# RWKV-6 attention and an MLP: products with A and with the state in two operations, standard deviation behind the MLP, a new order

## The chip, the cores and the metric

The kernel runs on one core of a Trainium2 chip, as one launch. The metric is the device time of one execution in microseconds (us), from three runs: lowest, median and highest. Beside them stands one execution taken by the hardware profiler.

## The reference

Two blocks follow each other. The first is a recurrence over time, for 4 batches and 8 heads of width 48, with 768 steps. Each head keeps a 48 x 48 state:

```python
for t in range(S):
    kt, vt, rt, wt = (k[:, :, t], v[:, :, t], r[:, :, t], w[:, :, t])
    cur = np.einsum('bhd,bhe->bhde', u[None] * kt, vt)
    y[:, :, t] = np.einsum('bhd,bhde->bhe', rt, state + cur)
    state = wt[:, :, :, None] * state + np.einsum('bhd,bhe->bhde', kt, vt)
```

The heads are then laid side by side (8 x 48 = 384 columns), and the second block is a residual MLP behind a layer norm without an offset, 384 to 1536 and back:

```python
xn = (x - mu) / np.sqrt(var + 1e-06) * g_ln
ch = np.maximum(xn @ w_ch1, 0.0) @ w_ch2
return x + ch
```

All data is fp32.

## The kernel before

**Rounds, units, tiles.** The work is cut into 8 rounds (4 batches x 2 halves of 384 steps). A round has two units of four heads, and three tiles of 128 steps; a tile holds two chunks of 64 steps for each head. Two heads lie on one tile's partitions, one on rows 0 to 47 and one on rows 64 to 111, so most products of the attention use a quarter of TensorE's array (48 or 64 rows by 48 to 64 columns), and four of them are put side by side. Such operations are called tiled here; a run of them is a burst. Round 0 is worked on in two parts, tile 0 and then tiles 1 and 2, to have the first results early (`parts_of_round`).

**The attention of a part** (`front`, L1675). `load` (L559) fetches w, k and r from HBM. `inner` (L583) forms on VectorE or GpSimd, in groups of four steps, what these steps do to each other (tiles `rk`, `pad_k`, `pad_r`, `nat_k`, `nat_w`, summed into `vals`), and `inner_by_tile` sends the sums through HBM into the layout of a masked copy. `turn` and `turn_w` transpose k, r and w on TensorE, ScalarE evicts them. Then come levels 2 to 5: at each, `quads` multiplies k by r for pairs of blocks of 4, 8, 16, 32 steps (PSUM tile `a`), `grow` (L850) multiplies k and r by the decay of a block on VectorE, and `keep` (L879) copies the wanted blocks of `a` into the matrix `A` (steps by steps, within a chunk) under a mask, on VectorE; `keep_last` does level 5 on ScalarE, and `place_own` puts the sums of `inner` on the diagonal. `turn_k` transposes k again, `load_v` fetches v, and a copy `vx` with the halves of the partitions swapped. `states` (L997) multiplies k by v for each chunk and scans the results into the states `s`, on VectorE.

**Outputs.** `outputs` (L1073) is one tiled operation for a unit. For each of its pairs of heads and tiles it issues four products with `A` (64 rows) and four products of r with the state (48 rows), which add up in one PSUM tile. Where both operands must lie on the same partitions as the result's other terms, it reads swapped copies: `rx` of r (made by `exchange_r`, L916) and `sx` of the state (made at the end of `states`), both on ScalarE, some 36 copies each in the whole kernel.

**Layer norm and MLP.** `normalize` (L1149) computes mean and variance on VectorE, the square root on ScalarE and the reciprocal on VectorE (`rstd`), and then xn = (x - mean) x rstd on VectorE. `turn_x` (L1219) transposes xn on TensorE, and ScalarE evicts it times g (`xf`). In round 0 the MLP's first product is in fp32 (`first_product`). From round 1 on it is made of three products in fp32r: operands are split into a high part, a low part and a difference (tiles `xhl`, `xd`; the weights `wh`, `wl`, and `d`, which is streamed from HBM by SP for each of the 12 column blocks). In rounds 4 to 7 the second product is split as well (`thirds`, L1461; `hH`, `hL`, `hD`). In the other rounds `mlp` (L1583) makes it in fp32 (PSUM tile `o`). VectorE adds the result to x, and SP stores it.

**The order.** No loop order of the program is the order of issue. Each piece is recorded with `plan.add`: which engines may do it and for how long, what it reads and writes, and which buffers it needs. `Plan.order` (L242) then walks a written list, `ORDER` (L76), of the recorded operations' numbers (plus 10000 where the second of the possible engines does it, 20000 for the third), gives each its buffers, and issues it. All engines issue in program order through one helper, `InOrder.call` (L47); so every instruction has line L47 in the profile, and is told by its tiles. Where the plan expects TensorE to wait for over 0.35 us and a bank of PSUM of kind `b` is free, it puts in products of zeros (`idle`, L1773), which nobody reads. `port` tells that VectorE and GpSimd are kept from working at the same time in such an operation.

**Start.** GpSimd builds the masks (`build_mask`, L486, and `build_own_mask`, L499) by selections on an index pattern and copies; VectorE clears `vals` and both PSUM tiles of kind `a`. The two buffers `A0` and `A1` are cleared once by an operation of the plan, on ScalarE, GpSimd or VectorE.

Of the kernel before, what the change touches and what calls it, by code (L numbers as in the profile page):

```python
# [55 lines left out]
class Op:  # L56
    def __init__(self, i, costs, fn, pri, lat, size, port, tiled, count):
        self.i, self.costs, self.fn, self.pri = i, costs, fn, pri
        self.lat, self.size, self.port, self.tiled, self.count = lat, size, port, tiled, count
        self.need, self.new, self.uses = set(), [], set()  # L60
        self.start = self.end = self.eng = None


class Plan:
# [177 lines left out]
    def order(self, busy, idle=None):  # L242
# [37 lines left out]
        for entry in self.ORDER:  # L280
# [55 lines left out]
            for n in op.uses:  # L336
                users[n] -= 1
                last[n] = max(last.get(n, 0.0), op.end)
                if not users[n]:
                    self.homes[self.tile_tag[n]].append((last[n] + self.RELEASE, self.place[n]))  # L340
# [1474 lines left out]
```

## Time and profile before

| what | value |
|---|---|
| three runs, lowest / median / highest | 489.94 / 490.76 / 492.56 us |
| profiled execution, own time | 490.19 us |
| its span, first to last instruction | 488.5 us |
| granted TensorE clock, mean | 1.000 |
| VectorE busy | 366.7 us (75%) |
| ScalarE busy | 274.0 us (56%) |
| GpSimd busy | 113.1 us (23%) |
| moved by DMA | 56.23 MB |

PE is TensorE's matmul, PEld its weight load, DVE VectorE, ACT ScalarE, POOL GpSimd, SP the engine that issues most transfers. A row of a timeline gives the start in the span, the busy time, the engine, line and operation, the tile written and those read with their shapes, the number of records, and, in brackets, the idle time ahead of it and what ended that. An fp32 product shows as two records. A row of the groups has the form, the number of records, their busy time and the mean of one in ns, and the idle time of the engine ahead of them.

### The profile page before, as it was taken

To read this page: it belongs to the slowest core of one execution; us is meant where nothing else is said; L and a number is where in the kernel's file an instruction comes from. 1 tells how busy PE (TensorE), PEld (TensorE's weight loads), DVE (VectorE), ACT (ScalarE), POOL (GpSimd) and SP (SyncE) were. 2 spreads that over 40 slices of the span, in tenths; PEclk is the share of its full clock that TensorE was granted. 3 is DMA by queue.
4 is the path that set the end of the run, shared out by engine and by line. 5 is a ranking of instruction groups with operands and counts; after the bars stand their busy time and mean duration, and the time that the engine had idled before them with its cause. 6 is when DMAs were issued, how large, how long until landed. Compare 5 with 4: busy or idle time off the path is not lost.

```text
span 488.5 us, 17306 instructions
## 1 busy us (share of the span) xinstructions
PE 477.8 (98%) x7412; PEld 410.4 (84%) x7412; DVE 366.7 (75%) x753; ACT 274.0 (56%) x624; POOL 113.1 (23%) x120
## 2 busy tenths in 40 slices
PE   8898999999999999999999999999999999999996
PEld 5676988767987778986699867799999999999996
DVE  6999999999966996875837998688887622732545
ACT  5779978943674256564064534779864444434430
POOL 4614013201602307404000610100141022121130
PEclk9999999999999999999999999999999999999999
DMA  7866777578452574461275403533411312223101
GB/s 210 237 174 148 205 176 171 163 177 218 126 150 75 96 208 94 115 186 39 70 201 140 90 3 58 109 116 85 125 34 60 88 47 65 66 66 98 64 1 49
DMA packets 105469, 56.23 MB, mean 115 GB/s; under 512 B 61872, under 2 KB 102320, under 8 KB 105392
## 3 DMA queue, kind: packets, MB, share of 16 engines
q1 hardware_dynamic: 105120, 54.92, 43.3%
q8 instruction: 58, 0.95, 0.9%
q10 hardware_dynamic: 272, 0.20, 0.1%
q14 instruction: 19, 0.16, 0.1%
HBM read 45.27 MB, written 7.47 MB: 108 GB/s over the span
## 4 chain that ended last, share of the span: by engine, by line
PE 87%; DVE 5%; SPq 1%; issue 1%; DMA 1%; DVEq 0%
PE h_ps L47 33%; PE a L47 23%; PE o L47 18%; PE o_2P L47 3%; PE r_ps L47 2%; PE o_2D L47 2%; PE xT_ps L47 2%; PE k_ps L47 2%; PE kn_ps L47 2%; SPq L47 1%; DVE A L47 1%; DVE s L47 1%; DVE x L47 1%; DVE k L47 1%; DMA d<-w1d 1%
## 5 line engine op out<-in xcount | busy, mean ns | idle before, releaser
L47 PE MATMUL o<-ffn,h 128*128 128x384 f32 x288 | 99.2, 488 | 0.0
L47 ACT ACTIVATE h<-h_ps 128x384 f32<-128x384 f32 (+2 forms) x108 | 47.7, 454 | 54.8 <-PE h_ps L47 54.2
L47 PEld LDWEIGHTS o<-ffn,h 128*128 128x128 f32 x288 | 52.3, 190 | 29.1
L47 ACT ACTIVATE h_ps<-h_ps 128x384 f32<-128x384 f32 x84 | 38.8, 475 | 49.0 <-PE h_ps L47 47.0
L47 DVE SCALAR_TENSOR_TENSOR hD<-hH,hL 128x384 fp32r<-128x384 f32 x48 | 30.4, 651 | 34.8 <-PE a L47 16.9
L47 PE MATMUL h_ps<-xd,d 128*128 128x384 f32 x204 | 50.0, 353 | 0.3 <-DMA d<-w1d 0.3
L47 PEld LDWEIGHTS a<-r,k 48*56 48x56 f32 (+3 forms) x3072 | 39.7, 122 | 10.1 <-issue 3.1
L47 POOL TENSOR_TENSOR hL<-h,hH 128x384 fp32r<-128x384 f32 x24 | 26.8, 1127 | 86.8 <-PE o_2D L47 21.1
L47 PE MATMUL a<-r,k 48*56 48x32 f32 (+3 forms) x3072 | 44.1, 208 | 1.1 <-DVE k L47 0.9
L47 PE MATMUL h_ps<-xhl,wl 128*128 128x384 f32 x180 | 43.8, 351 | 0.0
L47 DVE TENSOR_TENSOR k<-k,tot 112x768 f32<-112x768 f32 (+1 forms) x40 | 37.8, 947 | 5.9 <-PE a L47 4.5
L47 PE MATMUL h_ps<-xhl,wh 128*128 128x384 f32 x180 | 41.4, 338 | 0.0
L47 PEld LDWEIGHTS h_ps<-xd,d 128*128 128x128 f32 x204 | 35.4, 188 | 2.9 <-issue 0.9
L47 DVE TENSOR_TENSOR r<-r,tot 112x768 f32<-112x768 f32 (+1 forms) x40 | 34.1, 854 | 0.6 <-PE a L47 0.2
L47 PEld LDWEIGHTS h_ps<-xhl,wh 128*128 128x128 f32 x180 | 32.3, 188 | 0.0
L47 PEld LDWEIGHTS h_ps<-xhl,wl 128*128 128x128 f32 x180 | 31.0, 188 | 1.1 <-ACT h_ps L47 0.2
L47 PE MATMUL idle<-nought 128*128 128x384 f32 (+1 forms) x96 | 28.7, 425 | 1.0 <-DVE eps L47 1.0
L47 ACT ACTIVATE hH<-h 128x384 fp32r<-128x384 f32 x48 | 24.4, 522 | 8.0 <-PE a L47 3.5
L47 DVE COPY_PREDICATED A<-mask,a 128x768 f32<-128x768 int8 (+2 forms) x27 | 24.1, 893 | 5.6 <-PE a L47 5.5
L47 PE MATMUL h_ps<-xf,w 128*128 128x128 f32 (+1 forms) x144 | 26.0, 331 | 0.0
L47 PEld LDWEIGHTS idle<-nought 128*128 128x128 f32 x96 | 17.3, 200 | 9.1 <-issue 1.5
L47 DVE TENSOR_TENSOR hL<-h,hH 128x384 fp32r<-128x384 f32 x24 | 14.5, 606 | 13.7 <-PE o_2P L47 5.0
(180 smaller groups left out, 1171.2 us busy)
## 6 DMA issues: line engine op xcount, KB each, us to landing
d<-w1d SPq DMA_DIRECT2D x84, 192.0 KB, 2.8
raw<-in_moe_w_ch_dram SPq DMA_DIRECT2D x24, 384.0 KB, 3.9
nat_r<-in_r_dram SPq DMA_DIRECT2D x24, 192.0 KB, 4.0
nat_w<-in_w_dram SPq DMA_DIRECT2D x24, 192.0 KB, 4.2
v<-in_v_dram SPq DMA_DIRECT2D x24, 192.0 KB, 4.1
nat_k<-in_k_dram SPq DMA_DIRECT2D x23, 192.0 KB, 3.9
w1d<-w1diff SPq DMA_DIRECT2D x12, 192.0 KB, 3.4
out_dram<-x SPq DMA_DIRECT2D x4, 576.0 KB, 4.6
```

The source lines that it names most:

```text
L47: ins = self.tc.keep_in_program_order(f(*args, **kw))
```

## The change

In eight parts:

1. `exchange_r` and the swapped copy of the state are gone. `outputs` is split: `inside` issues the products with `A`, and `outputs` those of r with the state, now with the rows of r and of the state where they lie. Between both stands an operation of GpSimd, a memset of one element (`token`), which waits for the products with `A` and for which those with the state wait; `Op.after` adds these waits by hand.
2. xn is now mean - x, without rstd, and may be made on ScalarE or VectorE. g is negated once at the start. rstd multiplies the MLP's result in the addition of x; in rounds 4 to 7 ScalarE makes a second factor, `rstdD`. There are ten buffers for `rstd` in place of two.
3. The masks are made by VectorE from the identity, a maximum over blocks and a copy each. `vals` is cleared by GpSimd, and one of the PSUM tiles by ScalarE.
4. In `inner` the reads and writes of raw w, k and r are told apart by even and odd steps, and the padded buffers of round 0 are held from the start.
5. `keep` at level 4 may go to ScalarE, as four small copies.
6. The low part of `xf` may be made on GpSimd.
7. `idle` issues products of fp32r zeros of 512, 384 or 256 columns; before they were of fp32 zeros of up to 384. The zeros are written by ScalarE.
8. `ORDER` is a new list, of 2123 in place of 2158 operations; the clearing of `A` now has `port`, like the other operations that GpSimd may do.

The diff, without `ORDER` and the parts that only follow from the above:

```diff
+            others = [*others, *op.after]
...
-        "v": 1, "vx": 1, "s": 2, "last": 3, "rx": 2, "sx": 2, "x": 3, "xn": 3,
-        "xf": 2, "stats": 2, "mv": 2, "rstd": 2, "raw": 4, "rest": 32, "h": 12,
+        "v": 1, "vx": 1, "s": 2, "last": 3, "x": 3, "xn": 3,
+        "xf": 2, "stats": 2, "mv": 2, "rstd": 10, "raw": 4, "rest": 32, "h": 12,
...
-    zeros = nought.broadcast_to([P, P])
+    nought_r = const.tile([P, 1], F32R, name="nought_r")
+    ACT.copy(out=nought_r, in_=nought)
...
-    for t in kept["vals"] + a_homes:
-        DVE.memset(t, 0.0)
+    for t in kept["vals"]:
+        POOL.memset(t, 0.0)
...
+    DVE.memset(a_homes[0], 0.0)
+    ACT.copy(out=a_homes[1], in_=nought[:, :, None].broadcast_to([P, 2, 512]))
+
+    for lev in range(LOW, NLEV):
+        n = 1 << lev if lev < NLEV - 1 else Q
+        blocks = const.tile([P, C // (2 * n if lev < NLEV - 1 else n)], F32, name=f"blocks{lev}")
+        ones = ident.rearrange("p (h q two n) -> p q two h n", h=2, two=2, n=n)[:, :, 0] if (
+            lev < NLEV - 1
+        ) else ident.rearrange("p (h q n) -> p q h n", h=2, n=n)
+        DVE.tensor_reduce(out=blocks, in_=ones, axis=AX.XY, op=ALU.max)
+        m = masks[lev].rearrange("p (q n) -> p q n", n=n) if lev < NLEV - 1 else own_mask
+        DVE.tensor_copy(out=m, in_=blocks[..., None].broadcast_to(m.shape))
...
+        def go(e="DVE"):
             ps, to = squares(part, lev)
             ps = ps.rearrange("s b c (q n) -> s b c q n", n=n)
             to = to.rearrange("s b c (q two n) -> s b c q two n", two=2, n=n)[..., 1, :]
+            if e == "ACT":
+                for row in range(0, P, 2 * n):
+                    q = row // (2 * n) % (C // (2 * n))
+                    ACT.copy(out=to[ds(row, n), :, :, q], in_=ps[ds(row, n), :, :, q])
+                return
...
+        both = lev == NLEV - 2
...
-    def exchange_r(q, part):
-        rnd, c0, nc = part
-        uu = q % U
-        name = f"rx{q}"
-        for j in range(2):
-            def go(j=j):
-                if j == c0 == 0:
-                    tile_("rx", name, [P, NK, C])
-                R = tiles[f"r{rnd}"][:, uu].rearrange("p (r c i t) -> p r c i t", r=NP, i=2, t=C)
-                to = tiles[name].rearrange("p (r c) t -> p r c t", r=NP)
-                ACT.copy(
-                    out=to[ds(HP * (1 - j), D), :, c0 : c0 + nc],
-                    in_=R[ds(HP * j, D), :, c0 : c0 + nc, 1, :],
-                )
...
+    def inside(q, part):
+        rnd, c0, nc = part
+        uu, A_ = q % U, f"A{rnd % 2}"
 
         def go():
-            y = tile_("a", y_, [P, 2, 512])[:, :, 0 : NK * D].rearrange(
-                "p j (k e) -> p j k e", k=NK
-            )
-            A = a_bufs[rnd % 2]
-            for pr, c in tiles_of:
+            y, A = y_view(q, part), a_bufs[rnd % 2]
+            for pr, c in tiles_of(part):
                 k_ = pr * TT + c
                 for i in range(2):
                     for j in range(2):
@@ -1091,36 +1057,52 @@
                             y[ds(C * i, C), j, k_], A[rows, j, uu, k_, :],
                             tiles[f"vx{rnd}"][rows, uu * NP + pr, c] if j
                             else tiles[f"v{rnd}"][rows, uu * NH + 2 * pr, c],
-                            start=(pr, c) == tiles_of[0], stop=False, skip_group_check=True,
+                            start=(pr, c) == tiles_of(part)[0], stop=False, skip_group_check=True,
                         )
+
+        plan.add(
+            "PE", cost(part, 0.03, 0.73), go,
+            r=[(A_, lev, c0) for lev in range(LOW, NLEV - 1)] + [(A_, 0, c0, j) for j in range(2)]
+            + [(A_, NLEV - 1, c0, i, j) for i in range(2) for j in range(2)]
+            + [(f"vx{rnd}", c0), (f"v{rnd}", c0)],
+            w=[(y_of(q, part), "inside")], new=[("a", y_of(q, part))],
+            pri=urgent(part, 24) - 0.5, lat=0.2, tiled=True, count=32 * nc,
+        )
+        plan.add(
+            "POOL", 0.2, lambda: POOL.memset(token, 0.0), r=[(y_of(q, part), "inside")],
+            w=[(y_of(q, part), "token")], pri=urgent(part, 24) - 0.4, port=False,
+        ).after.append(plan.ops[plan.writer[y_of(q, part), "inside"]])
...
-                        if i:
-                            R, s = tiles[rx][rows, k_], tiles[sx][rows, pr, c]
-                        elif c:
-                            R, s = Rn, tiles[s_][rows, pr, 2 * c - 1]
+                        rows = ds(HP * j, D)
+                        if i or c:
+                            s = tiles[s_][rows, pr, 2 * c - 1 + i]
                         elif before is not None:
-                            R, s = Rn, tiles[before][rows, pr]
+                            s = tiles[before][rows, pr]
                         else:
                             continue
                         PE.matmul(
-                            y[ds(C * i, C), j, k_], R, s,
+                            y[ds(C * i, C), j, k_], tiles[f"r{rnd}"][rows, uu, ds((2 * k_ + i) * C, C)], s,
...
+            r=[(y_, "token"), (s_, c0), (s_, 0)] + keys_of("r", part, [uu]) + ([before] if before else []),
+            w=[y_], new=[(x_tag(rnd), x_)] if uu == c0 == 0 else [],
+            pri=urgent(part, 24), lat=0.2, tiled=True, count=32 * nc - 16 * (before is None and c0 == 0),
+        ).after.append(plan.ops[plan.writer[y_, "token"]])
...
+        def shrunk():
+            ACT.activation(
+                out=tile_("rstd", f"rstdD{rnd}", [P, TT]), in_=tiles[rs_], func=AF.Copy, scale=-1 / (1 + E12)
+            )
+
+        def apply(e, i):
             t = tile_("xn", f"xn{rnd}_{i}", [P, RN])
-            DVE.tensor_scalar(
-                out=t, in0=tiles[x_][:, i].rearrange("p h d -> p (h d)"),
-                scalar1=tiles[mv_][:, i, 0:1], scalar2=tiles[rs_][:, i : i + 1],
-                op0=ALU.subtract, op1=ALU.mult,
-            )
+            x, mean = tiles[x_][:, i].rearrange("p h d -> p (h d)"), tiles[mv_][:, i, 0:1]
+            if e == "ACT":
+                ACT.activation(out=t, in_=x, func=AF.Identity, bias=mean, scale=-1.0)
+            else:
+                DVE.tensor_scalar(out=t, in0=x, scalar1=mean, scalar2=-1.0, op0=ALU.subtract, op1=ALU.mult)
...
-        def low():
+        def low(e):
             Hx, Lx, _ = x_parts(rnd, kc)
-            DVE.tensor_tensor(out=Lx, in0=tiles[xf], in1=Hx.bitcast(F32), op=ALU.subtract)
+            BY[e].tensor_tensor(out=Lx, in0=tiles[xf], in1=Hx.bitcast(F32), op=ALU.subtract)
...
-                    scalar=-WHOLE / E12, in1=x, op0=ALU.mult, op1=ALU.add,
+                    scalar=tiles[f"rstdD{rnd}"][:, i : i + 1], in1=x, op0=ALU.mult, op1=ALU.add,
...
-            def relu(h_=h_, ps=ps, scale=WHOLE if rnd < LAST else 1.0):
+            def relu(h_=h_, ps=ps, scale=WHOLE if rnd < LAST else WHOLE**2):
...
-                DVE.tensor_tensor(
+                DVE.scalar_tensor_tensor(
                     out=tiles[x_][:, i], in0=tiles[o].rearrange("p (h d) -> p h d", d=D),
-                    in1=tiles[x_][:, i], op=ALU.add,
+                    scalar=tiles[f"rstd{rnd}"][:, i : i + 1], in1=tiles[x_][:, i],
+                    op0=ALU.mult, op1=ALU.add,
...
+        "ACT", 0.2, lambda: ACT.activation(out=g_sb, in_=g_sb, func=AF.Copy, scale=-1.0), w=["g"], pri=-9,
...
-        while n:
-            now = min(n, TT)
+        cols = 512 - 128 * (n % 3)
+        for _ in range(max(n * 576 // (cols + 38), 1)):
             PE.matmul(
-                t[:, 0 : now * P], zeros, nought.broadcast_to([P, now * P]), start=True, stop=True
-            )
-            n -= now
+                t[:, 0:cols], nought_r.broadcast_to([P, P]), nought_r.broadcast_to([P, cols]),
+                start=True, stop=True,
+            )
```

More of the change, by code (lines that the diff above doesn't have):

```diff
@@ L59, in __init__ @@
         self.lat, self.size, self.port, self.tiled, self.count = lat, size, port, tiled, count
-        self.need, self.new, self.uses = set(), [], set()
+        self.need, self.new, self.uses, self.after = set(), [], set(), []
         self.start = self.end = self.eng = None
@@ L465 @@
     own_mask = const.tile([P, C // Q, Q], I8, name="mask_own")
-    plan.hold("sx", "wide")
-    wide_ = tile_("sx", "wide", [P, NP, TT, D]).rearrange("p r c d -> p (r c d)").bitcast(I8)
-    wide = {lev: wide_[:, ts(lev, C)] for lev in range(LOW, NLEV - 1)}
-    wide[0] = wide_[:, 0 : P // Q]
     for i in range(FC):
@@ L574, in load @@
             plan.add(
-                queue, 0.64, lambda c=c: go(c), w=[(name, c)],
+                queue, 0.64, lambda c=c: go(c), w=[(name, c, i) for i in range(2)],
                 new=[("n" + nm, name)] if rnd and c == 0 else [],
@@ L625, in inner @@
             apart_one, lambda: k_()[:, 0::2], lambda: r_()[:, 1::2], half, 0.0,
-            r=raw["k"] + raw["r"], w=[rk], new=[("rk", rk)],
+            r=even["k"] + odd["r"], w=[rk], new=[("rk", rk)],
         )
@@ L629, in inner @@
             lambda: padded("k", part)[:, 0::2], lambda: k_()[:, 0::2], lambda: w_()[:, 1::2],
-            half, 0.1, r=raw["k"] + raw["w"], w=pad["k"][:1], new=[] if c0 else [("pk", f"pad_k{rnd}")],
+            half, 0.1, r=even["k"] + odd["w"], w=pad["k"][:1], new=[("pk", f"pad_k{rnd}") for _ in first_pad],
         )
@@ L891, in go @@
             )
+        both = lev == NLEV - 2
         plan.add(
-            "DVE", cost(part, 0.155, 0.98), go,
-            r=[(name, 0), (name, 1), ("mask", lev), (f"A{rnd % 2}", "nought")],
+            ("DVE", "ACT") if both else "DVE",
+            (cost(part, 0.155, 0.98), 4 * cost(part, 0.217, 0.539)) if both else cost(part, 0.155, 0.98), go,
+            r=[(name, 0), (name, 1), (f"A{rnd % 2}", "nought")],
             w=[(f"A{rnd % 2}", lev, c0)], pri=urgent(part, 10.5 + 2 * lev),
@@ L1071, in states, with y_of, tiles_of, y_view @@
         return before
-    def outputs(q, before, part):
+    token = const.tile([1, 1], F32, name="token")
+    def y_of(q, part):
+        return f"y{q}_{part[1]}"
+    def tiles_of(part):
+        return [(pr, c) for pr in pairs for c in range(part[1], part[1] + part[2])]
+    def y_view(q, part):
+        return tile_("a", y_of(q, part), [P, 2, 512])[:, :, 0 : NK * D].rearrange(
+            "p j (k e) -> p j k e", k=NK
+        )
+    def inside(q, part):
         rnd, c0, nc = part
-        uu = q % U
-        b, f, g = units[q]
-        y_, x_, sx, s_, rx = f"y{q}_{c0}", f"x{rnd}", f"sx{q}", f"s{q}", f"rx{q}"
-        tiles_of = [(pr, c) for pr in pairs for c in range(c0, c0 + nc)]
+        uu, A_ = q % U, f"A{rnd % 2}"
         def go():
-            y = tile_("a", y_, [P, 2, 512])[:, :, 0 : NK * D].rearrange(
-                "p j (k e) -> p j k e", k=NK
-            )
-            A = a_bufs[rnd % 2]
-            for pr, c in tiles_of:
+            y, A = y_view(q, part), a_bufs[rnd % 2]
+            for pr, c in tiles_of(part):
                 k_ = pr * TT + c
@@ L1552, in thirds @@
             if last:
-                plan.add("DVE", 0.558, add, r=[keys[1]] + whole, w=[(x_, "sum", i)], pri=EVICT)
-                plan.add("DVE", 0.558, rest, r=[keys[0], (x_, "sum", i)], w=[(x_, "out", i)], pri=EVICT)
+                plan.add("DVE", 0.558, add, r=[keys[1], f"rstdD{rnd}"] + whole, w=[(x_, "sum", i)], pri=EVICT)
+                plan.add("DVE", 0.558, rest, r=[keys[0], (x_, "sum", i), (f"rstd{rnd}", 0)], w=[(x_, "out", i)], pri=EVICT)
                 plan.add("SP", 0.6, store, r=[(x_, "out", i)], pri=EVICT, lat=2.2, size=0.69, count=1)
@@ L1698, in front @@
                 plan.add(
-                    ("ACT", "POOL", "DVE"), (1.5, 1.8, 1.75), clear, w=[(f"A{i}", "nought")], pri=-40, port=False
-                )
-            plan.add("POOL", 1.72, build_own_mask, r=["wide"], w=[("mask", 0)], pri=-40, port=False)
-            for lev in range(LOW, NLEV - 1):
-                plan.add(
-                    "POOL", 1.5, lambda lev=lev: build_mask(lev), r=["wide"], w=[("mask", lev)],
-                    pri=lev - 40, port=False,
+                    ("ACT", "POOL", "DVE"), (1.5, 1.8, 1.75), clear, w=[(f"A{i}", "nought")], pri=-40
                 )
```

103 lines of the change are left out of this document (34 added, 69 removed), and 251 rows, old and new, of the table ORDER.

## Prediction

> **What bounds the kernel now.** I read the page first, then the stretches, the waits of TensorE, and the timelines of the first 50 us.
>
> ```profile
> PE 477.8 (98%) x7412; PEld 410.4 (84%) x7412; DVE 366.7 (75%) x753; ACT 274.0 (56%) x624; POOL 113.1 (23%) x120
> ...
> PE   8898999999999999999999999999999999999996
> ...
> PEclk9999999999999999999999999999999999999999
> ```
>
> TensorE is busy for 98% of the span at full clock, so this looks like a kernel that only less TensorE work can shorten. The next view cuts the span at 50.3 us, where the outputs of the first round end. Its columns are the stretch, its length, and busy time of PE, PEld, DVE, ACT and POOL.
>
> ```profile
> 0.00:50.30 50.30, 44.13 (x803) 32.11 (x803) 45.21 (x119) 36.46 (x82) 21.21 (x41) 1.00 0.72 192
> 50.30:120.00 69.70, 69.70 (x1231) 54.92 (x1228) 67.97 (x144) 50.41 (x125) 9.53 (x9) 1.00 0.71 182
> 120.00:484.30 364.30, 363.99 (x5401) 323.37 (x5392) 252.37 (x490) 187.16 (x419) 82.37 (x70) 1.00 0.36 91
> ```
>
> The same cut, for the instructions that write the tile `idle` alone:
>
> ```profile
> 0.00:50.30 50.30, 28.34 (x94) 17.03 (x94) 1.00 0.72 192
> ```
>
> So 28.34 of the 44.13 busy us in the head are fillers, products of zeros that nobody reads, and 6.17 us more are idle. Only about 16 of the first 50 us are work. After 50.3 us TensorE never rests: 0.3 us is missing in 434. The longest wait stands in the head, and the only one far behind it is short:
>
> ```profile
> PE w_ps L47 <- POOL w L47: 1.2, 1, 1.2
> ...
> PE h_ps L47 <- DMA d<-w1d: 0.3, 1, 0.3
> ```
>
> In the head VectorE is the limit. It idles until its second product has its data, and then runs on to the masked copies that the last outputs of round 0 wait for:
>
> ```profile
> 4.66 0.36 DVE L47 TENSOR_TENSOR rk<-nat_k,nat_r 128x192 f32<-128x192 f32 x1 [1.20 <-DMA nat_k<-in_k_dram]
> 6.52 0.36 DVE L47 TENSOR_TENSOR pad_k<-nat_k,nat_w 128x192 f32<-128x192 f32 x1 [1.50 <-DMA nat_w<-in_w_dram]
> ...
> 46.15 2.09 DVE L47 COPY_PREDICATED A<-mask_own,va 128x512 f32<-128x512 int8 x2
> ```
> ```profile
> 48.30 0.25 PE L47 MATMUL a<-vx,A 64*64 64x48 f32 x1 [0.58 <-DVE A L47]
> ```
>
> The kernel is therefore a head of 50 us set by VectorE, 434 us of TensorE without a gap, and a tail of 4.4 us.
>
> **The change part by part.** The profiled execution took 490.19 us, of which 488.5 us are its span; the runs shown have a median of 490.76. I work out a difference and take it from the median.
>
> *TensorE's products.* The same 4444 products stand in both programs, in the same shapes. The products with A and those of r with the state only move into two operations, and those that read swapped copies now read the originals. That is 0 us, if a quarter of the array serves a product as well whichever half of the rows it reads; the rows of the two kinds differ by nothing that this trace shows. What differs is fillers, changes of kind, and waits.
>
> *Fillers.* Before: 26 of 384 columns and 22 of 128 in 23 groups, in fp32. After: 52 of 512, 17 of 384 and 24 of 256 in 15 groups, in fp32r. In the chain six records of `o` are three fp32 products of 384 columns, and six of `h_ps` in the last rounds are six fp32r products:
>
> ```profile
> 161.91 1.94 PE o L47 x6
> ...
> 360.16 1.06 PE h_ps L47 x6
> ```
>
> So 0.65 us and 0.18 us. Scaled by columns (an estimate), the old fillers come to 26 x 0.65 + 22 x 0.22 = 21.7 us, the new ones to 52 x 0.23 + 17 x 0.18 + 24 x 0.12 = 17.9: **3.8 us less**. With 15 places in place of 23 where a filler runs short, the 6.17 us of idle shrink by a third at most, 2.1 us. Against that the first filler now needs a zero that ScalarE writes behind its table load:
>
> ```profile
> 0.80 1.28 ACT L47 ACT_TABLE_LOAD   x1 [0.80 <-PEq L1799]
> 2.10 0.20 ACT L47 ACTIVATE root<-eps 128x1 f32<-128x1 f32 x1
> ```
> ```profile
> 0.99 6.81 PE L47 MATMUL idle<-nought 128*128 128x384 f32 x16 [0.99 <-DVE eps L47]
> ```
>
> It starts at about 2.3 in place of 0.99 us. The old first group, 7 wide ones and one narrow, took 6.81 us where 4.8 is the price above: the array was slow at first. [...] The late start is worth 0 to 1.3 us, as later groups take it up or not; I take 0.6. By this count the head gains 3.8 + 2.1 - 0.6 = 5.3 us, between 3.8 - 1.3 = 2.5 and 5.9.
>
> *VectorE's queue in the head.* This is the other count. The first load of w is now the first transfer that SP issues; before it was the third:
>
> ```profile
> 0.81 1.43 SPq L47 DMA_DIRECT2D nat_r<-in_r_dram  x2
> ...
> 2.29 0.61 SPq L47 DMA_DIRECT2D nat_w<-in_w_dram  x1
> ```
>
> The loads of r and k had landed by 4.66 us. So VectorE starts in earnest near 4.9 in place of 6.52: 1.6 less. It makes the masks itself (eight small operations on the identity) while it waits for loads. To the last operation ahead of the outputs of round 0 stood 109 instructions, now 101: copies at level 4 go to ScalarE, three products to GpSimd, the normalization to ScalarE; by the starts of like rows 2.4 us less. Behind it TensorE had both products left (48.30 to 50.2), now only those with the state: 0.9 less. And 1.7 us more of real products are done by then (transposes of round 1 come earlier). Together **6.6 us**. A check further on, at the second product group of round 1, which waits for this r:
>
> ```profile
> 59.76 0.95 DVE L47 TENSOR_TENSOR r<-r,tot 112x768 f32<-112x768 f32 x1
> ```
> ```profile
> 61.60 1.37 PE a L47 x96
> ```
>
> Before, VectorE had some 50 us of work to there and 4.2 us of stalls from 6.52 on; now 45.2, so 4.9 + 45.2 + 4.2 = 54.3, with 1.2 us less of TensorE's work done: 61.6 - 54.3 - 1.2 = 6.1. I take 6.0 for the head, over the 5.3 of the fillers, since fillers are only placed where a bank is free.
>
> *Swapped copies.* They were ScalarE's:
>
> ```profile
> L47 ACT COPY rx<-r 48x384 f32<-48x384 f32 x28 | 14.1, 510 | 0.6
> ...
> L47 ACT COPY sx<-s 48x288 f32<-48x288 f32 x28 | 11.8, 430 | 4.1 <-DVE s L47 3.7
> ```
>
> That is 25.9 us, and 3 us in small forms, off an engine at 56%: 0 us, except in the head, where it is counted. 17 of these take their place, at ScalarE's rates:
>
> ```profile
> L47 DVE TENSOR_SCALAR xn<-x,mv,rstd 128x384 f32<-128x384 f32 x24 | 10.6, 475 | 0.1
> L47 DVE TENSOR_TENSOR xhl<-xf,xhl 128x384 fp32r<-128x384 f32 x15 | 8.2, 550 | 0.6 <-ACT xhl L47 0.6
> ```
>
> Nine of the 19 of the second kind (with `xk`) go to GpSimd. The standard deviation behind the MLP lets transposes start without square root and reciprocal; behind 50 us TensorE waits for neither: 0. Its factor rides in additions that are made anyway: 0.
>
> *Bursts of small products.* TensorE pays to come back from one. The product group behind a burst takes 2.13, without one 1.94 (quoted above):
>
> ```profile
> 157.89 1.45 PE a L47 x96
> 159.34 2.13 PE o L47 x6
> ```
>
> From the first product of the MLP on there are 39 bursts before and 43 after: 4 x 0.19 = **+0.8 us**.
>
> *The token.* Each of 18 output pairs now has a round trip: the products with A end, GpSimd writes one element, the products with the state start. No row shows that trip. Its parts are near: a product ends some 0.22 us behind its last issue (the 0.25 of the row at 48.30), GpSimd's smallest write takes
>
> ```profile
> 7.03 0.14 POOL L47 MEMSET wide<- 128x64 int8 x1
> ```
>
> so some 0.45 us with two hops. In the order of the new program 0.48 us or more of other products stand between, in all pairs but one: **+0.5**, bounds 0 and 18 x 0.45 = 8. Behind a token that waits stand GpSimd's next products, and VectorE behind those.
>
> *Tail.* VectorE ends last:
>
> ```profile
> 482.80 1.03 DVE x L47 x2
> ...
> 483.85 1.03 DVE x L47 x2
> ...
> 484.91 0.56 DVE x L47
> ```
>
> The last tile is now the one whose two sums are operations of their own, so its first addition starts under the last two products: -0.2.
>
> The sum: -6.0 + 0.8 + 0.5 - 0.2 = -4.9, that is 485.3 on the profiled execution's own time and **485.9** on the median.
>
> [...] While GpSimd multiplies, a VectorE product of 0.41 us takes 1.24 and ends behind it:
>
> ```profile
> 34.81 1.24 DVE L47 TENSOR_TENSOR k<-k,tot 112x256 f32<-112x256 f32 x1
> ```
> ```profile
> 34.36 1.41 POOL L47 TENSOR_TENSOR pad_k<-nat_k,nat_w 128x576 f32<-128x576 f32 x1 [1.50 <-DVE s L47]
> ```
>
> [...] GpSimd gets more such products, some ten of them between 50 and 110 us.
>
> **The rivals.**
> 1. *The gain is given back between 50 and 110 us.* VectorE was busy there for 67.97 of 69.70 us, and TensorE's order now runs closer behind it. Ten more products of GpSimd that each hold it up by 0.3 us are 3 us: 488.9. Against it: VectorE's list to round 2 is 7 us and more shorter.
> 2. *The head doesn't get shorter.* Loads land no earlier, or the static fillers hold TensorE up: 2.5 in place of 6.0, so 489.4. For it: the late first filler. Against it: both counts.
> 3. *Slower: the token waits for GpSimd.* GpSimd works in order, and a product like the 1.41 us above can stand ahead of a token. If it is late by 1.1 us at half of the 18, TensorE, which had no gap, loses 10 us: 495.8. It outweighs the gain from 0.27 us a token. Against it: GpSimd is at 23%, and work stands between most pairs.
>
> **How the numbers follow.** The forecast has 0.62, rival 1 0.16, rival 2 0.11, rival 3 0.11. The range goes from 483.0 (a head of 7.3, a free token, half the bursts) to 490.5 (past rivals 1 and 2); left out are rival 3 and some 0.05 more. A measurement of this kernel can tell about 0.5% from no change, 488.3 to 493.2. Faster by more: the forecast and a good third of rivals 1 and 2, 0.75; within it: the rest of those, 0.14; slower: 0.11.
>
> **What would show it.** The outputs of round 0 end near 45 in place of 50.2 us, VectorE's first product with w starts at 4.9, fillers take some 18 us plus the slow start. TensorE rests under 1 us after the head, with 43 bursts. Rival 1 would show as waits of `a` on VectorE's k or r between 50 and 110 us; rival 2 as outputs of round 0 still near 49; rival 3 as waits of `a` on GpSimd's token. A gap of over 2 us behind the head makes the prediction wrong.

## The result and the profile after

The changed kernel takes 493.13 us (491.56 to 496.80), the kernel before 490.07 in the same session. The ratio is **1.0066, 95% interval 1.0046 to 1.0085**: 3.1 us slower. Forecast were 485.9 us and a range of 483.0 to 490.5. The profiled execution took 492.70 us with a span of 490.9, against 490.19 and 488.5.

From the page of the changed kernel: busy times, and the transfers of instructions (queue, pieces, MB, share of the DMA engines), which the prediction didn't look at.

```profile
PE 475.5 (97%) x7409; PEld 410.1 (84%) x7409; DVE 352.4 (72%) x727; ACT 257.5 (52%) x593; POOL 126.0 (26%) x136
...
q8 instruction: 58, 0.95, 0.8%
```

TensorE is busy for 2.3 us less than before, and the span is 2.4 us longer. So it rests more, 15.4 us in place of 10.7. The same cut as in the prediction, at the end of round 0's outputs, which is now 47.8 us:

```profile
0.00:47.80 47.80, 41.32 (x818) 33.42 (x818) 42.77 (x118) 38.27 (x88) 13.26 (x29) 1.00 0.79 209
47.80:120.00 72.20, 71.57 (x1345) 56.46 (x1340) 70.09 (x137) 50.50 (x125) 20.95 (x19) 1.00 0.69 173
120.00:485.90 365.90, 362.56 (x5254) 320.27 (x5252) 237.96 (x473) 168.77 (x383) 91.77 (x88) 1.00 0.35 91
```

and the fillers within the first stretch:

```profile
0.00:47.80 47.80, 22.24 (x93) 16.29 (x93) 1.00 0.79 209
```

The fillers fell from 28.34 to 22.24 us, and the head did get shorter. But behind it TensorE rests for 0.6 and 3.3 us, where it rested for 0.3 in all before. Its waits name only part of that, and the largest behind the head is put down to nothing ("issue"):

```profile
PE idle L47 <- ACT nought_r L47: 2.3, 1, 2.3
PE a L47 <- issue: 2.2, 2, 1.5
...
PE a L47 <- DVE s L47: 0.8, 2, 0.5
...
PE h_ps L47 <- DVE x L47: 0.7, 1, 0.7
```

To see where the two kernels part, I gave every product that isn't a filler its usual time from start to start (the same in all traces: 9 to 16 ns for a record of a tiled product, the others as priced in the prediction), and added up what was done by a given moment. The lead over the kernel before, in us, from one trace each (so differences of some tenths mean nothing):

| at us | 50 | 80 | 120 | 170 | 220 | 260 | 365 |
|---|---|---|---|---|---|---|---|
| changed kernel | 4.0 | 4.0 | 3.0 | 3.0 | 2.2 | 0.4 | -1.3 |
| e2, fp32 fillers | 3.8 | 2.9 | 1.9 | 1.7 | 1.6 | 1.2 | 0.2 |
| e6, before with 64 instructions more | 0.8 | 1.1 | 0.8 | 1.5 | -4.2 | -3.4 | -8.2 |
| e8, e2 and last round | 4.5 | 4.4 | 3.3 | 3.3 | 3.2 | 2.7 | 1.9 |
| e12, e8 and two moves | 3.0 | 2.1 | 1.9 | 1.2 | 0.9 | 0.6 | -0.2 |

The head gained 4.0 of the 6.0 us forecast. All of it and more is lost behind it: 1.0 by 120 us, 1.8 between 220 and 260, and so on, until TensorE ends at 485.90 against 484.26, and VectorE behind it takes longer too.

The largest single loss, in the timeline of TensorE in the changed kernel, and the transfers of instructions just then (the row of a view of the stretch from 221.5 to 223.3 us, in which the data queue took 91.5% of the DMA engines):

```profile
221.08 1.52 PE L47 MATMUL a<-r,k 48*60 48x32 f32 x96
222.42 0.64 PE L47 MATMUL a<-v,k 64*48 64x48 f32 x40
224.54 0.30 PE L47 MATMUL a<-v,k 64*48 64x48 f32 x8 [1.48 <-issue]
```
```profile
q1 hardware_dynamic: 733, 0.43, 91.5%
q8 instruction: 1, 0.02, 5.8%
```

TensorE stops in the middle of one operation, whose operands lie in tiles that the records ahead of it had read as well, and goes on at 224.54. In the trace a piece of its program is on the way from 221.54 to 223.20: the product goes on 1.3 us behind its end and 3.0 us behind its start. The page says how large a piece is: 58 pieces for 2 x 7409 records (a product's record and one of its weight load), that is 255 instructions, 0.95 MB / 58 = 16 KB each. The second rest in a burst is of 0.72 us, up to 328.53, and its piece is on the way from 325.91. From the one to the other it is 17 pieces and 4330 records, again 255 a piece.

**Theory.** TensorE's instructions arrive in such pieces of some 255, and the plan reckons with 256 (`PIECE = 256`). A burst uses one up in 1.2 to 2 us (128 records of a product, 9 to 16 ns each, with a weight load each), less than the 3.0 us from the start of that piece to the next product (2.2 to 3.3 at the other rests). Whether a burst is hit depends on where the cuts between pieces fall in it. `Plan.order` works out where they fall (`fetches`) and counts instructions, for the fillers by `count += 4 * -(-n // 3)`, a line that the diff leaves alone. That is right for fp32 fillers (four instructions a product: the 48 of the kernel before left 96 records of products and 96 of weight loads), and comes to 124 for the 15 groups. The new `idle` issues 93 products of two (93 and 93 records): 186. So all cuts behind the head lie 62 instructions from where the order was planned with. **Rival:** the two rests are chance, and the loss is that of the new order: waits for VectorE, more bursts, the token.

### The profile page after: what moved, and what is told of

It is laid out like the page before. It is cut to its first block, busy times and chain, and to the rows that moved or that the text cites. A ratio compares the mean times of both kernels' runs of the same rounds, so it can differ in the third digit from the quotient of the medians.

```text
span 490.9 us, 17279 instructions
## 1 busy us (share of the span) xinstructions
PE 475.5 (97%) x7409; PEld 410.1 (84%) x7409; DVE 352.4 (72%) x727; ACT 257.5 (52%) x593; POOL 126.0 (26%) x136
## 4 chain that ended last, share of the span: by engine, by line
PE 81%; DVE 11%; issue 2%; ACT 2%; DMA 1%; SPq 1%; POOL 1%; DVEq 0%; POOLq 0%
PE h_ps L47 27%; PE a L47 23%; PE o L47 19%; PE o_2P L47 3%; PE k_ps L47 2%; DVE A L47 2%; PE o_2D L47 2%; PE r_ps L47 2%; PE xT_ps L47 2%; DVE vals L47 2%; DMA raw<-in_moe_w_ch_dram 1%; DVE s L47 1%; PE kn_ps L47 1%; SPq L47 1%; DVE nat_k L47 1%
## 5 line engine op out<-in xcount | busy, mean ns | idle before, releaser
L47 PE MATMUL o<-ffn,h 128*128 128x384 f32 x288 | 100.4, 490 | 0.0
L47 POOL TENSOR_TENSOR hL<-h,hH 128x384 fp32r<-128x384 f32 x24 | 25.7, 1078 | 89.2 <-ACT hH L47 32.9
L47 DVE TENSOR_TENSOR k<-k,tot 112x768 f32<-112x768 f32 (+1 forms) x40 | 31.5, 790 | 12.3 <-PE a L47 12.1
L47 DVE TENSOR_TENSOR hL<-h,hH 128x384 fp32r<-128x384 f32 x24 | 13.8, 584 | 27.6 <-ACT hH L47 14.6
L47 ACT COPY A<-a 32x384 f32<-32x384 f32 (+5 forms) x60 | 25.3, 426 | 7.2 <-PE a L47 5.4
L47 ACT ACTIVATE xf<-xT_ps,g_sb 128x384 f32<-128x384 f32 (+2 forms) x27 | 14.5, 547 | 27.1 <-PE xT_ps L47 20.4
L47 ACT ACTIVATE hH<-h 128x384 fp32r<-128x384 f32 x48 | 23.4, 518 | 6.9 <-issue 4.9
L47 POOL TENSOR_TENSOR nat_r<-pad_k,pad_r 128x576 f32<-128x576 f32 (+1 forms) x9 | 15.0, 1668 | 40.5 <-DVE nat_k L47 38.3
```

The costliest lines, as they stand in the source:

```text
L47: ins = self.tc.keep_in_program_order(f(*args, **kw))
```

## The experiments

All twelve in one table; medians in us, of the kernel before as measured beside each, and the ratio with its 95% interval. The ratio is taken over all runs and isn't the quotient of the two medians, which would be 1.0033 in e1. There are 12 runs of each, but 6 of e4 and 4 of e6, and 29 of the kernel before (17 beside e12).

| run | edit | median | before | ratio |
|---|---|---|---|---|
| e1 | changed kernel again | 492.94 | 491.31 | 1.0052 (1.0026 to 1.0078) |
| e2 | fp32 fillers | 491.13 | 491.31 | 0.9997 (0.9976 to 1.0019) |
| e3 | 194 instructions more | 490.86 | 491.31 | 0.9994 (0.9973 to 1.0014) |
| e4 | 128 instructions more | 496.15 | 491.31 | 1.0107 (1.0065 to 1.0150) |
| e5 | e2, no zero by ScalarE | 490.15 | 490.10 | 1.0014 (0.9995 to 1.0034) |
| e6 | before, 64 instructions more | 502.16 | 490.10 | 1.0255 (1.0220 to 1.0290) |
| e7 | e2, low parts on VectorE | 491.52 | 490.10 | 1.0018 (0.9994 to 1.0042) |
| e8 | e2, last round's factor in xn | 489.80 | 490.10 | 0.9988 (0.9972 to 1.0004) |
| e9 | e2, e5 and e8 together | 490.16 | 490.37 | 0.9995 (0.9978 to 1.0012) |
| e10 | changed kernel, zero by VectorE | 493.22 | 490.37 | 1.0070 (1.0041 to 1.0098) |
| e11 | e2, a longer token | 491.36 | 490.37 | 1.0024 (1.0006 to 1.0042) |
| e12 | e8, two moves in the order | 490.76 | 491.69 | 0.9985 (0.9965 to 1.0004) |

### e1 to e4: where the cuts fall

e1 is the changed kernel unaltered.

> The changed kernel once more, unaltered, with a second profile, so that the others of this group have it beside them. Fetch theory: the two rests of TensorE in the middle of a burst of small products, 1.48 us at 222.9 and 0.72 us at 327.6, which the waits put down to nothing, come again at the same products, since they hang on where the 256-instruction pieces of TensorE's program are cut. Rival (chance, a disturbed transfer): they are somewhere else or not there. Either way the time is some 3 us above the kernel before.

e2 has the old fillers in the new places:

```diff
-        cols = 512 - 128 * (n % 3)
-        for _ in range(max(n * 576 // (cols + 38), 1)):
-            PE.matmul(
-                t[:, 0:cols], nought_r.broadcast_to([P, P]), nought_r.broadcast_to([P, cols]),
+        while n:
+            now = min(n, TT)
+            PE.matmul(
+                t[:, 0 : now * P], nought.broadcast_to([P, P]), nought.broadcast_to([P, now * P]),
...
+            n -= now
```

> Only the fillers are put back: fp32 zeros, up to 384 columns, one group in the same 15 places, 124 instructions of TensorE in all in place of 186, the number that the order was planned with. Fetch theory: all cuts behind the head move by 62 instructions to where the plan has them, and the rests in bursts go: TensorE rests under 1 us behind the head, and the time falls by 2.6 us (1.67 and 0.93 us, the surplus of those two) up to 5, to 488 to 490.5. Rival (the loss is that of the order itself, waits for VectorE and more bursts): the time stays within 1 us of the unaltered one, or rises by what wider fillers hold up.

e3 and e4 keep the new fillers and add small ones to the first group (e3: 52 for 7; e4: 35 for 6):

```diff
+    extra = [52]
     def idle(n, home):
-        cols = 512 - 128 * (n % 3)
-        for _ in range(max(n * 576 // (cols + 38), 1)):
+        cols, small = 512 - 128 * (n % 3), extra.pop() if extra else 0
+        for _ in range(max(n * 576 // (cols + 38), 1) - 7 * (small > 0)):
...
+        for _ in range(small):
+            PE.matmul(
+                t[0:32, 0:32], nought.broadcast_to([P, 32]), nought.broadcast_to([P, 32]),
+                start=True, stop=True,
+            )
```

> The new fillers stay, but in the first group 7 of the 28 wide ones give way to 52 of 32 columns by 32 in fp32, so that TensorE has 194 instructions more in the head: with the 62 that the fillers have over the plan that is 256, one whole piece, so the cuts fall again where the plan has them. Fetch theory: the same as with the fp32 fillers, 2.6 to 5 us less than unaltered. Rival: no change beyond 1 us.

> The same with 35 small ones for 6 wide ones, 128 instructions more: the cuts fall 190 behind the plan's. Fetch theory: other bursts are hit, three to six rests of 1 to 2.3 us, at other places than 222.9 and 327.6, and the time is 2 to 6 us above the unaltered one. Rival: no change beyond 1 us.

Measured: e1 rests behind the same two records, the 40th and the 34th of their runs, 1.02 us behind the product that starts at 223.58 and 0.45 behind that at 327.90. So their place is no chance, though their size varies from run to run (e10, with the same cuts, has the first with 1.75 us and not the second). With the cuts back in place, by two different means, the time falls by 0.55% and 0.58% (1.0052 against 0.9997 and 0.9994, 2.7 and 2.9 us; by the medians 1.8 and 2.1), and with the cuts elsewhere it rises by 0.55% (1.0107; 3.2 us by the medians). e2 came out above the 488 to 490.5 us that were expected, at 491.13. The one line that tells it, from TensorE's waits in e1, e2, e3 and e4:

```profile
PE a L47 <- issue: 1.5, 2, 1.0
```
```profile
PE a L47 <- issue: 0.8, 2, 0.6
```
```profile
PE a L47 <- issue: 0.3, 1, 0.3
```
```profile
PE a L47 <- issue: 4.3, 4, 1.6
```

What is left in e2 and e3 stands elsewhere: 0.57 us at 66.4 and 0.3 in the head in e2, 0.31 at 57.9 in e3. So the planned cuts don't free every burst. In e4 the rests stand in other operations, for instance in the product groups at 142 and 263 us:

```profile
143.93 0.35 PE L47 MATMUL a<-r,k 48*60 48x32 f32 x10 [1.42 <-issue]
```
```profile
265.34 1.42 PE L47 MATMUL a<-r,k 48*60 48x32 f32 x45 [1.56 <-issue]
```

The rival would have had all four within 1 us, and it falls for the two rests. For the rest, that nothing is left of the gain of the head, it stays open, since e2 and e3 are no faster than before.

### e6: the kernel before, shifted

In the first group of the old fillers 17 small fp32 products stand for one wide one, 64 instructions more and nothing else.

> The kernel before, with 64 instructions of TensorE more in its first group of fillers (17 small fp32 products for one wide one, 0.65 us of work either way), nothing else. Fetch theory: the kernel before has no rest behind its head only because its plan counts the instructions rightly; shifted by a quarter of a piece it gets three to six rests of 0.5 to 2 us in bursts of small products, and is 3 to 10 us slower. Rival (the sensitivity is that of the new order alone): within 1 us of before.

Measured: 1.0255, **12 us slower**, above what was expected. TensorE's waits, and the longest one in its timeline:

```profile
PE a L47 <- issue: 6.0, 4, 2.6
```
```profile
176.88 0.43 PE L47 MATMUL a<-r,k 48*60 48x32 f32 x8 [2.61 <-issue]
```

So the run without a gap that the prediction took for a property of the kernel hangs on the exact number of instructions in the head. That profile is of the fastest of its four runs (498.37 us); e4's is of the slowest of its six (499.49 us).

Beside the longest of these rests the clock was lower, which the waits don't show. The clock that TensorE was granted, from the pages of e4 and e6 (tenths of full speed, slices of 12.4 us):

```profile
PEclk9999999999989999999997999999999999999999
```
```profile
PEclk9999999999999979999999999999999999999999
```

In e6 it is 0.50 from 175.9 to 182.7 us, beside the rest of 2.61 us, and in e4 0.50 from 145.5 to 148.9 and 0.51 from 264.9 to 271.8, beside its rests of 1.42 and 1.56 us; the means of these two executions are 0.993 and 0.99. That the rests bring the clock down was not shown. The profile of the changed kernel has no such stretch from its head to TensorE's end, but its mean clock is under 0.997 in 12 of 32 runs (the first 20 and e1), which take some 2 us more than the rest, against 1 of 24 in e2 and e3 and 2 of 29 in the kernel before beside them. So up to 0.8 us (an estimate, 12 of 32 runs times 2 us) of what the rests cost on average may be the clock. No run separates the two.

### e5, e10: the load of k

In e5 the fp32r zero, which nothing reads with fp32 fillers, is left out; in e10 the fillers stay as changed and VectorE writes it.

```diff
-    ACT.copy(out=nought_r, in_=nought)
+    DVE.tensor_copy(out=nought_r, in_=nought)
```

> On the kernel with the fp32 fillers (491.1 us, first run): the fp32r zero that ScalarE writes at the start, which nobody reads there, is left out. Theory: that write and the second table load it brings stand ahead of the first load of k on ScalarE's queue; k was issued at 2.02 us in place of 1.01, and VectorE's first product of round 0 started at 6.06 in place of 4.66. Without it the load is issued near 1.0 again, VectorE starts near 4.9, and since VectorE sets the head, the outputs of round 0 end 1.0 to 1.3 us earlier and the time falls by as much. Rival (another load or ScalarE sets the head): VectorE starts earlier, and waits as much more further on; the time stays within 0.3.

> The changed kernel with one edit: VectorE writes the fp32r zero, so ScalarE has one table load and the load of k ahead of its other work; the fillers stay fp32r, and so does the shift of the cuts by 62 instructions. Theory: VectorE's first product at 4.9 to 5.0, outputs of round 0 end 1 to 1.5 us earlier, the rests in bursts near 222 and 327 stay: 1 to 1.5 us under the unaltered one, 1.5 above before. Rival: the earlier first filler needs no earlier load, nothing changes.

The start of ScalarE in the changed kernel; ACTq are its issues of transfers. The load of k is issued with the copy to `nought_r`, which starts when the first table load is done. The second table load starts only behind that, so it isn't what holds this load up, as the expectation of e5 has it:

```profile
0.72 1.28 ACT L47 ACT_TABLE_LOAD   x1 [0.72 <-PEq L1789]
2.02 0.19 ACT L47 CAST nought_r<-nought 128x1 fp32r<-128x1 f32 x1
2.02 0.72 ACTq L47 DMA_DIRECT2D nat_k<-in_k_dram  x1
2.23 1.28 ACT L47 ACT_TABLE_LOAD   x1
```

VectorE's stalls in the first 12 us, in the changed kernel and in e10:

```profile
6.06 0.36 DVE L47 TENSOR_TENSOR rk<-nat_k,nat_r 128x192 f32<-128x192 f32 x1 [2.63 <-DMA nat_k<-in_k_dram]
...
11.05 0.56 DVE L47 TENSOR_TENSOR pad_k<-nat_k,nat_w 128x384 f32<-128x384 f32 x1 [0.61 <-DMA nat_k<-in_k_dram]
```
```profile
4.83 0.36 DVE L47 TENSOR_TENSOR rk<-nat_k,nat_r 128x192 f32<-128x192 f32 x1 [1.27 <-DMA nat_r<-in_r_dram]
...
10.99 0.56 DVE L47 TENSOR_TENSOR pad_k<-nat_k,nat_w 128x384 f32<-128x384 f32 x1 [1.51 <-DMA nat_k<-in_k_dram]
```

The first half of the theory holds: without the zero on ScalarE the load is issued at 0.93 (e5) and 1.11 (e10), and the first product starts at 5.01 and 4.83. The second half falls. VectorE stops again where it needs the second load of k, 10.99 against 11.05 us, and e10's ratio (1.0070) is that of the changed kernel (1.0052 to 1.0066). In e5's trace that load happened to land 0.8 us earlier than in e2, and the lead at 50 us was 5.5 instead of 3.8; but that was the fastest of its twelve runs, and the median shows nothing. The loads set the head, and their arrival varies from run to run (VectorE goes on with the second k at 9.83 us in e5, at 10.59 in e2). e10 also rests for 0.53 us in a burst at 65.7, where the changed kernel doesn't.

### e8: the last additions

Round 7 alone: square root and reciprocal ahead of xn, xn times rstd on VectorE, and constants in the last six additions.

```diff
-                    scalar=tiles[f"rstdD{rnd}"][:, i : i + 1], in1=x, op0=ALU.mult, op1=ALU.add,
+                    scalar=tiles[f"rstdD{rnd}"][:, i : i + 1] if rnd < NR - 1 else -1 / (1 + E12), in1=x, op0=ALU.mult, op1=ALU.add,
...
-                    scalar=tiles[f"rstd{rnd}"][:, i : i + 1], in1=x, op0=ALU.mult, op1=ALU.add,
+                    scalar=tiles[f"rstd{rnd}"][:, i : i + 1] if rnd < NR - 1 else 1.0, in1=x, op0=ALU.mult, op1=ALU.add,
```

> On the kernel with the fp32 fillers: in round 7 alone the standard deviation goes into xn again (on VectorE), and the six last additions have constants for factors. Theory: an addition with a factor per row takes 0.62 us, 0.64 from start to start, with a constant 0.56 and 0.53; six stand in a row at the end, so the stretch from TensorE's end to VectorE's end falls from 1.7 to near 1.2 us, and the time by 0.5. Rival (the order of the last tiles makes the tail): it stays at 1.7.

The last additions in the changed kernel, and in e8:

```profile
483.92 0.62 DVE L47 SCALAR_TENSOR_TENSOR x<-a,rstdD,x 128x384 f32<-128x384 f32 x1 [2.64 <-PE a L47]
484.57 0.62 DVE L47 SCALAR_TENSOR_TENSOR x<-a,rstd,x 128x384 f32<-128x384 f32 x1
485.11 0.61 DVE L47 SCALAR_TENSOR_TENSOR x<-a,rstdD,x 128x384 f32<-128x384 f32 x1
485.75 0.62 DVE L47 SCALAR_TENSOR_TENSOR x<-a,rstd,x 128x384 f32<-128x384 f32 x1
486.28 0.61 DVE L47 SCALAR_TENSOR_TENSOR x<-o_2D,rstdD,x 128x384 f32<-128x384 f32 x1
487.00 0.62 DVE L47 SCALAR_TENSOR_TENSOR x<-o_2P,rstd,x 128x384 f32<-128x384 f32 x1
```
```profile
481.16 1.61 DVE L47 SCALAR_TENSOR_TENSOR x<-a,x 128x384 f32<-128x384 f32 x3
482.69 0.55 DVE L47 SCALAR_TENSOR_TENSOR x<-o_2D,x 128x384 f32<-128x384 f32 x1
483.34 0.56 DVE L47 SCALAR_TENSOR_TENSOR x<-o_2P,x 128x384 f32<-128x384 f32 x1
```

With a factor per row an addition takes 0.62 us, with a constant 0.55, and the six are a chain. From TensorE's end to VectorE's it is 1.72 us in the changed kernel, 1.20 in the one before, 1.27 in e8: the theory holds, for 0.45 us. In the median that is too little to be seen apart (0.9988 against 0.9997).

### e7, e11, e12: the rest of the loss

e7 takes the nine low parts of `xf` off GpSimd (their entries in `ORDER` less 10000).

> On the kernel with the fp32 fillers: the nine low parts of xf that went to GpSimd are made by VectorE again (0.55 us each there, 0.95 to 1.1 on GpSimd), in the same places of the order. Theory that GpSimd's products hold VectorE up where it is short: the wait of 0.7 us for x at 122 us goes and the time falls by 0.5 to 1.5. Rival (VectorE's own list is what is late there): two or three more products ahead of that addition make the wait longer, and the time rises by up to 1.

Measured: 1.0018, no gain. The wait for x at 122 us shrank from 0.7 to 0.3, and one of 1.3 us for another of VectorE's additions came up at 298 us. Neither reading is confirmed.

e11 makes the token `[P, 384]` in place of `[1, 1]`.

> On the kernel with the fp32 fillers: GpSimd's token is a memset of 128 by 384 (0.42 us by the like row of the start) in place of one element (0.09), so each of the 18 round trips is 0.33 us longer. If the token were on TensorE's path at every pair, the time would rise by 18 x 0.33 = 6 us. Theory (other products cover it at all but the first four pairs): by at most 1.3 us, and TensorE waits for a token only in the head.

Measured: 1.0024 against 0.9997 for e2, some 1.3 us, the most that the theory allowed; 6 us lie far outside both intervals. TensorE's waits for the token in e11, both in the first 49 us:

```profile
PE a L47 <- POOL token L47: 0.6, 2, 0.4
```

e12 moves, in `ORDER` of e8, round 2's sum 676 behind the scans 541 and 539, and the addition 407 ahead of 861:

> On the kernel with fp32 fillers and the last round's standard deviation in xn (e8): two moves in VectorE's order. The scans of round 1 go ahead of a sum of round 2 (1.33 us) behind which TensorE's products with A waited 0.3 us (0.5 with what goes with it), and round 0's last addition to x goes ahead of three products of later rounds, behind which TensorE's h_ps waited 0.7 us (0.86). Theory (between 80 and 130 us the head's lead is lost to VectorE's order): both waits go, and the time falls by 1 to 1.4 us under e8, to 0.996 of before. Rival (what was moved back is waited for in its turn): the same time as e8, with new waits of TensorE between 80 and 180 us.

What it aims at, VectorE and GpSimd in the changed kernel:

```profile
118.34 1.75 DVE L47 TENSOR_TENSOR nat_w<-nat_w 128x576 f32<-128x576 f32 x1
120.02 1.34 DVE L47 TENSOR_TENSOR nat_k<-nat_k,nat_r 128x1152 f32<-128x1152 f32 x1
121.28 0.54 DVE L47 SCALAR_TENSOR_TENSOR wl<-wh,w 128x384 fp32r<-128x384 f32 x1
121.75 0.60 DVE L47 SCALAR_TENSOR_TENSOR x<-o,rstd,x 128x384 f32<-128x384 f32 x1
```
```profile
118.06 1.42 POOL L47 TENSOR_TENSOR rk<-nat_k,nat_r 128x576 f32<-128x576 f32 x1 [1.01 <-DVE A L47]
```

The addition that frees TensorE's bank is fourth in VectorE's list, and the first of the list takes 1.75 us beside GpSimd's product (0.75 for the like product at 36.8 us, without one). Measured in e12: both waits are gone, and a new one stands behind them:

```profile
132.43 0.43 PE L47 MATMUL r_ps<-ident,pad_r 128*112 128x128 f32 x2 [1.03 <-POOL pad_r L47]
```

The ratio is 0.9985, against 0.9988 for e8. The rival holds: what is moved ahead here is waited for at the next place. e9 joins e2, e5 and e8:

> The changed kernel with three edits: fp32 fillers, no zero written by ScalarE, and the last round's standard deviation in xn. Theory (fetch, late load and last additions are three separate losses of 2.6, 1.2 and 0.5 us): 4.3 us under the unaltered one, that is 1.5 to 2.5 under the kernel before: 487.5 to 489. Rival (they overlap, or something else takes the gain back): within 1 us of before.

Measured: 0.9995, 490.16 us, above the 487.5 to 489 expected. Of the three losses only the fetch is seen in the times. No version here beats the kernel before by more than its interval.

## Why the prediction was wrong

**The direction** failed at the step *Fillers*: they were priced by time alone, 3.8 us less, and "What differs is fillers, changes of kind, and waits" leaves out that they are instructions too. 62 more of them than the plan counts cost 2.7 us (e1 against e2 and e3), and none of the three rivals had that. It turns an equal time into a slower one; why it isn't the forecast gain of 4.9 us lies in the head, the waits behind it and the tail, below. The page of the kernel before shows its instructions coming in pieces (`q8 instruction`, 58 of them there too), and the prediction had counted the fillers of both programs, but not what the plan takes them for. The claim that TensorE "never rests" was true of one alignment only (e6). A piece is 16 KB, 255 instructions by the count of records, and single rests of up to 2.61 us were measured in bursts of small products (e6).

**The head**, 4.0 us against 6.0 (some 2.3 to 5.5 in the traces of the new order). The count by fillers gave 5.3, between 2.5 and 5.9, and holds within its bounds, but by luck in part: the fillers fell by 6.1 us (28.34 to 22.24) and not by 3.8, and the idle time of the head grew from 6.17 to 6.48 where 2.1 less was counted. The 28.34 us had been shown and were priced at 21.7 and a slow start. The 0.6 us for the late first filler was the author's estimate, and no run shows it: records of fp32 fillers of 384 columns followed each other in 0.64 us until 4.4 us before, and in 0.32 from 4.8 on; those of 512 in fp32r in the changed kernel in 0.43 until 5.0, and in 0.22 from 5.4 on. Where the first filler starts at 1.1 in place of 2.3 us (e10), the time is no shorter (1.0070). The count by VectorE's queue failed at "So VectorE starts in earnest near 4.9": the load of k came behind a table load, so VectorE started at 6.06, and its first product with w at 6.34 in place of 6.52; and where it started at 4.83 the second load took it back (e10). Fewer instructions on VectorE were worth what the loads left of it.

**Products** at 0: right. In unbroken runs of output products a record starts 14.6 ns behind the one ahead of it before (192 records with A and the state mixed), and 14.7 after, with A and with the state alike (96 each), whichever half of the rows they read.

**Bursts**, +0.8: right, as far as two traces show. There are 43 bursts, before 39, as counted. Behind the head that is 86 changes between small products and others, before 78; their surplus over the usual spacing is some 9.6 against 8.7 us, 0.9 more.

**Token**, +0.5: small, as forecast, and a little high. TensorE waited for it for 0.2 us in e3, and not at all that shows in the changed kernel. Rival 3 did not happen.

**Tail**, -0.2: wrong by 1.0. It is 0.8 us longer, 0.5 of it VectorE's (e8), the rest the last store. The step that failed is "Its factor rides in additions that are made anyway: 0": with a factor per row they take 0.62 us in place of 0.55, six in a row.

**Waits behind the head** failed as well: "behind 50 us TensorE waits for neither: 0" was said of square root and reciprocal, and the sum has a term for no other wait than the token's. They cost some 2 us, the longest 0.70 us for VectorE's addition to x at 122. That is **rival 1** (the gain given back between 50 and 110 us) come true in part: 1.0 us by 120, 0.9 more at 122. In the rows at 118 us (under e12) a VectorE product takes 1.75 us (0.75 for the like product at 36.8 us) and ends behind GpSimd's, like the row at 34.81 us in the prediction, 1.24 us. These are single rows; what holds VectorE's product up was not shown. And VectorE's list was late by its own order too, and e7 and e12 show that taking single waits away moves them.

Together, from one trace of each: 4.0 gained; lost 2.6 at the two rests (0.2 more than their idle time each, counted from start to start), some 2.4 at short waits for VectorE and others, of which before had 0.4, 0.9 in bursts, 0.8 in the tail. That is 2.3 slower, where the spans differ by 2.4 and the medians by 3.1. Without the rests the new order equals the old one (e2, e3). That 0.9 and 2.4 are causes was read from traces and is not shown: no experiment undid the bursts, and those that moved single waits (e7, e12) gained nothing.

## What to carry to other kernels

In this kernel, with its bursts of products of 9 to 16 ns a record, the number of instructions ahead of a burst was part of its timing: 64 more cost 12 us (e6), 62 more than planned 2.7 us (e1 against e2 and e3). In a kernel like it, look at the transfers of instructions on the page, and take any edit that adds or drops instructions, fillers among them, for a possible move of all cuts behind it. A plan that counts instructions has to be told when an operation changes its count. And a gapless engine is worth a second look at what keeps it gapless: a small shift of the kernel before (e6) would have said more than its profile.

## What the runs showed of the hardware that was not expected

- 64 instructions more in the head, with no more work, cost the kernel before 12 us (1.0255), and the changed kernel gained 2.9 from 194 more (2.1 by the medians).
- Beside rests of 1.42 to 2.61 us in a burst TensorE's granted clock fell to 0.50 or 0.51 for 3.4 to 6.9 us (e4, e6); beside others of 1.28 to 1.75 us it didn't (e6, e10, the changed kernel).
- With a copy to fp32r on ScalarE ahead of a square root stood two table loads of 1.28 us there, without it one (the changed kernel, the one before), and the load of k on ScalarE's queue was issued 1.0 us later (2.02 against 1.01).
- An addition with a factor per row takes 0.61 to 0.62 us for 128 x 384, with a constant 0.55 to 0.56.
